# Four layers of attention on one core: two weight loads moved behind the opening stage, a dearer load in the planner, and a newly searched order

## The chip, the cores and the metric

The kernel is one program on one core of a Trainium2 chip. The core has a matrix engine (PE; its weight loads have a row of their own, PEld), a vector engine (DVE), a scalar engine (ACT), GpSimd (POOL) and SyncE (SP), which here does nothing but issue DMAs. Each engine takes its instructions in the order written, and waits for others at semaphores. The metric is the device time of one execution in microseconds (us); 495.82 us is the median of three runs of the kernel before (495.67 to 497.61).

## The reference

A token block x of 2048 x 512 (bf16) goes through two rounds of two layers, each added to x:

```python
x = A_x
x = x + _A_ref(_layernorm(x, axis=-1), A_wq, A_wk, A_wv, A_wo, A_beta)
x = x + _B_ref(_layernorm(x, axis=-1), B_wqkv, B_w_phi, B_wo)
x = x + _A_ref(_layernorm(x, axis=-1), A_wq, A_wk, A_wv, A_wo, A_beta)
x = x + _B_ref(_layernorm(x, axis=-1), B_wqkv, B_w_phi, B_wo)
```

Layer A is attention with a memory: 32 heads of width 16, four segments of 512 tokens. In each segment it forms q, k and v, takes a causal softmax attention within the segment, mixes it by a gate with what a running memory (a sum over earlier segments of phi(k) times v) returns for phi(q), and multiplies the result by `A_wo`. Layer B is linear attention: q and k are each multiplied per head by a 16 x 16 matrix `w_phi`, softmaxes of the product and of its negative are the features, and features of all keys times v are summed over all 2048 tokens before any query is answered; the result is multiplied by `B_wo`.

## The kernel before

**Stages.** x stays on the core as sixteen tiles `X` of 128 tokens. For each of four segments the program does: layer norm (`ln`: statistics on DVE, line 1099, the root on POOL, line 1105, the scaling on DVE, line 1114), a transpose of the normed tile `xn` into `xnT`, the projections of layer A (`a_proj`: keys `KT` and `KTo` for even and odd heads, queries `QT`, values `VT`, and `PhiK`/`PhiQ`), attention in pairs of tiles (`a_att`: score matmuls, exponentials of 1024 columns on ACT in lines 1289, 1300 and 1310, masks on POOL in line 1316 and DVE in line 1320, the product with `VT`), the output projection (`a_out`, `WA_o`), then layer B's norm, keys (`b_keys`: `WB_k`, `WB_v`, exponentials `Ek`) and queries (`b_queries`). Layer B's output (`b_out`, `WB_o`) can begin only when all four segments have gone through `b_keys`. Then the second round does the same, its first stage lying beside the end of the first round.

**The opening stage.** Before the first segment the inputs come in. `setup` issues the first four tiles of x and the weights of layer A in halves on the queues of ACT and SP; `late_loads` (line 1030) issues the rest on SP: the other twelve tiles of x, `w_phi`, the raw q and k weights of layer B (into the tiles `EQ`), `WA_o`, the value weight `WB_v` and the output weight `WB_o` of layer B, 512 KB each. `fold_weights` (line 1070) multiplies layer B's q and k weights by `w_phi` once, into `WB_q` and `WB_k`: each of eight 128-row pieces of `EQ` is transposed by a DMA into a tile `OT` (`transposed`, line 867; the DMA itself is line 860), multiplied on PE with the block matrix `wbd` (a tile `O`), and copied out of PSUM by ACT or DVE.

**The queue of SP.** All transposes by DMA, all loads on SP and all stores stand in one queue in a fixed order. A transpose waits at its place until the engine that makes its input has done so, and everything behind it waits too. In this trace what SP issues in the opening lands in the order of its issue.

**What sets the order.** Nothing is written out in the order in which it runs. `Program.add` records each operation with what it reads and writes; `PLAN` gives each of the 3474 operations its rank, `sequence` makes one list of them that respects the dependences, and each engine gets its part of the list. `ON` says for operations that could run on ACT, DVE or POOL which one takes them. `schedule` then walks through the lists with a cost for each operation: it decides which tile of a pool and which PSUM bank an operation gets, and puts idle matmuls (`warm`, line 1585) on PE where it expects a gap of at least one of them or where the share of time that PE is busy in the last `WIN` = 3.4 us would fall below `LOW`. `PAIRS` names score matmuls that are issued interleaved with the ones behind them. A DMA has a cost on the queue that issues it (0.5 us for a load, 1.28 for a transpose, line 863), a time on the rings (`weight`), and an `at`, the earliest time at which the planner lets it start. `at` puts no wait into the program: what is left of it on the chip is the DMA's place in the order.

The functions that the change touches:

Of the kernel before, what the change touches and what calls it, by code (L numbers as in the profile page):

```python
# [31 lines left out]
LOW = 0.39  # L32
# [11 lines left out]
    165, 213, 219, 241, 255, 269, 275, 281, 293, 297, 299, 307, 319, 325, 563, 585, 591, 609, 627, 670, 694, 696, 698, 702, 720, 722, 724, 728, 734,  # L44
    746, 748, 754, 961, 963, 985, 991, 1003, 1021, 1027, 1039, 1068, 1070, 1074, 1082, 1094, 1100, 1102, 1108, 1120, 1124, 1128, 1134, 1146, 1148,
    1150, 1152, 1154, 1351, 1392, 1410, 1422, 1451, 1455, 1465, 1477, 1481, 1505, 1511, 1517, 1529, 1531, 1533, 1537, 1543, 1784, 1790, 1844, 1868,
    1870, 1874, 1900, 1906, 1922, 1924, 1926, 1932, 1944, 1948, 1950, 1952, 2215, 2245, 2269, 2292, 2294, 2296, 2298, 2300, 2322, 2326, 2350, 2352,
    2370, 2378, 2384, 2639, 2651, 2657, 2669, 2687, 2693, 2718, 2730, 2748, 2756, 2774, 2776, 2794, 2796, 2800, 2802, 3021, 3023, 3046, 3064, 3082,
    3123, 3151, 3157, 3163, 3181, 3183, 3207, 3215, 3331, 3333,
# [8 lines left out]
    0, 5, 1, 6, 41, 43, 10, 8, 12, 11, 60, 27, 7, 66, 30, 29, 34, 31, 49, 350, 115, 44, 75, 65, 74, 83, 68, 94, 42, 16, 15, 26, 17, 25, 18, 22, 14,  # L58
    13, 62, 46, 48, 73, 80, 63, 106, 54, 55, 39, 121, 99, 67, 96, 118, 51, 57, 64, 32, 76, 56, 85, 72, 21, 78, 24, 71, 82, 89, 92, 70, 58, 28, 79,
    133, 135, 137, 111, 101, 151, 169, 181, 180, 38, 47, 35, 45, 37, 36, 33, 52, 50, 87, 97, 90, 77, 110, 53, 9, 122, 102, 91, 130, 120, 140, 40, 59,  # L60
    104, 81, 206, 244, 290, 142, 109, 23, 95, 134, 108, 143, 103, 107, 154, 124, 2, 164, 128, 69, 160, 177, 88, 131, 114, 158, 201, 196, 229, 217,
    153, 282, 295, 171, 231, 197, 243, 198, 175, 84, 148, 98, 19, 20, 147, 344, 353, 366, 360, 376, 157, 4, 112, 113, 179, 3, 105, 182, 168, 183, 193,
    172, 149, 185, 210, 208, 187, 163, 207, 209, 235, 212, 184, 191, 218, 273, 204, 248, 224, 144, 155, 245, 256, 253, 292, 268, 239, 289, 166, 116,
    226, 165, 214, 260, 286, 246, 194, 188, 213, 284, 265, 215, 324, 200, 343, 340, 351, 358, 294, 216, 269, 304, 328, 330, 335, 319, 312, 323, 308,
    342, 367, 354, 241, 384, 394, 402, 389, 364, 438, 454, 434, 442, 274, 211, 310, 270, 337, 336, 278, 141, 203, 242, 311, 288, 317, 258, 232, 297,
    322, 267, 375, 176, 349, 383, 281, 327, 387, 380, 396, 406, 414, 371, 400, 261, 411, 325, 359, 238, 392, 178, 390, 233, 422, 401, 298, 315, 357,
    374, 329, 386, 339, 326, 363, 420, 382, 399, 431, 447, 436, 279, 412, 262, 479, 368, 437, 362, 421, 369, 473, 487, 449, 453, 419, 285, 468, 403,
    443, 474, 501, 504, 481, 510, 450, 440, 537, 558, 497, 506, 518, 240, 482, 478, 466, 280, 472, 439, 503, 528, 441, 448, 470, 455, 524, 477, 569,
    559, 522, 575, 584, 579, 616, 433, 661, 673, 614, 634, 205, 234, 129, 86, 220, 223, 299, 159, 252, 117, 174, 152, 125, 127, 186, 170, 222, 93,
    332, 150, 355, 348, 318, 408, 361, 195, 250, 397, 385, 372, 356, 381, 266, 404, 410, 484, 499, 461, 415, 391, 416, 398, 379, 377, 202, 428, 427,  # L70
    417, 345, 407, 145, 429, 432, 313, 247, 287, 493, 446, 425, 395, 489, 430, 517, 451, 471, 476, 418, 465, 502, 459, 346, 293, 271, 277, 513, 512,
    333, 500, 494, 458, 539, 444, 485, 555, 561, 556, 545, 593, 625, 393, 365, 409, 136, 192, 126, 119, 199, 259, 219, 237, 291, 307, 296, 309, 283,
    228, 254, 139, 146, 306, 303, 320, 314, 331, 347, 316, 321, 457, 464, 452, 463, 475, 460, 490, 276, 492, 300, 638, 690, 644, 699, 688, 645, 715,
    630, 717, 632, 531, 520, 538, 542, 435, 567, 469, 649, 534, 519, 456, 547, 530, 557, 554, 580, 585, 551, 566, 553, 532, 495, 774, 787, 526, 650,
    769, 793, 755, 752, 801, 797, 808, 796, 788, 602, 651, 764, 677, 779, 726, 802, 800, 768, 833, 848, 851, 838, 850, 871, 855, 866, 863, 1339, 1313,
    1166, 1172, 1290, 1284, 1048, 1247, 1275, 1265, 1150, 1209, 1352, 1341, 1424, 1317, 1580, 1434, 1459, 1064, 1634, 1543, 1632, 1641, 647, 657, 671,
    730, 639, 680, 540, 710, 721, 693, 703, 564, 598, 563, 562, 582, 488, 508, 509, 511, 521, 523, 491, 480, 533, 334, 544, 560, 424, 496, 570, 445,
    586, 576, 568, 594, 606, 505, 591, 467, 610, 612, 583, 543, 572, 529, 622, 574, 552, 426, 629, 615, 603, 635, 654, 666, 601, 498, 643, 617, 483,
    627, 587, 516, 648, 590, 652, 664, 663, 682, 678, 675, 549, 691, 653, 588, 641, 637, 667, 656, 676, 619, 659, 697, 662, 668, 685, 621, 636, 705,
    701, 698, 738, 613, 708, 804, 813, 825, 744, 577, 514, 605, 527, 679, 548, 620, 486, 707, 550, 735, 660, 696, 525, 669, 700, 716, 728, 686, 592,  # L80
    681, 757, 713, 714, 718, 689, 758, 766, 782, 785, 658, 611, 794, 626, 749, 694, 628, 573, 720, 571, 781, 772, 776, 736, 751, 684, 771, 759, 795,
    665, 816, 805, 829, 832, 843, 834, 820, 824, 791, 798, 810, 783, 831, 823, 830, 837, 799, 864, 754, 780, 809, 822, 778, 777, 733, 731, 875, 868,
    880, 807, 881, 872, 883, 899, 845, 692, 846, 859, 890, 727, 844, 762, 888, 885, 878, 817, 722, 672, 750, 737, 775, 773, 917, 877, 847, 927, 884,
    876, 842, 536, 608, 999, 957, 1012, 993, 156, 100, 264, 301, 272, 251, 373, 370, 352, 123, 162, 167, 189, 255, 161, 275, 305, 138, 515, 388, 581,
    578, 541, 600, 546, 646, 607, 640, 655, 985, 988, 936, 840, 1003, 943, 742, 748, 765, 642, 674, 624, 597, 702, 338, 719, 723, 596, 740, 711, 747,
    695, 767, 784, 595, 589, 623, 790, 729, 763, 341, 806, 631, 818, 760, 743, 819, 828, 683, 839, 873, 841, 599, 604, 633, 704, 709, 724, 741, 745,
    753, 670, 761, 609, 867, 869, 378, 803, 897, 865, 712, 725, 706, 786, 835, 836, 734, 739, 746, 849, 792, 857, 756, 976, 947, 980, 974, 932, 1004,
    954, 860, 992, 1051, 903, 931, 821, 934, 920, 961, 1086, 1033, 968, 905, 963, 909, 904, 770, 858, 894, 889, 946, 915, 910, 925, 916, 1089, 1092,
    862, 955, 1140, 1102, 1043, 1110, 1088, 1044, 1101, 1090, 1065, 930, 1046, 1122, 1135, 1096, 1097, 1123, 1145, 1126, 1205, 1104, 1181, 1200, 1234,
    1212, 1098, 1094, 965, 986, 1118, 1108, 972, 891, 1115, 1148, 938, 973, 1163, 1159, 1197, 1210, 1198, 1187, 1136, 1078, 1263, 1268, 1572, 1435,  # L90
    1034, 1063, 1056, 1158, 1130, 1151, 1129, 1156, 1127, 1149, 1157, 902, 861, 907, 896, 852, 1079, 941, 1000, 967, 1084, 919, 1077, 1105, 1007,
    1008, 1072, 970, 1070, 1062, 1016, 939, 1053, 1054, 1038, 1083, 1138, 1117, 1107, 913, 1100, 1125, 1066, 1057, 1142, 923, 1144, 1128, 1047, 1112,
    1168, 1164, 1184, 1193, 1119, 1173, 1196, 1215, 1171, 1133, 1194, 1055, 1155, 978, 1190, 1203, 1177, 1175, 1223, 1162, 1229, 1232, 1189, 1141,
    1217, 1206, 1180, 1174, 1170, 1236, 1199, 1216, 1204, 1191, 1231, 1176, 1226, 1201, 1235, 1253, 1182, 1160, 1147, 959, 1041, 1296, 1311, 1314,
    1299, 956, 949, 900, 882, 995, 908, 998, 1013, 982, 983, 971, 811, 912, 887, 854, 964, 945, 826, 911, 898, 893, 906, 1006, 1009, 1005, 997, 1025,
    535, 1058, 926, 1029, 870, 1030, 1031, 1021, 987, 1017, 1024, 950, 928, 1018, 962, 944, 937, 1042, 892, 1035, 1068, 922, 1037, 1045, 1026, 1080,
    901, 1116, 1109, 1052, 1001, 1111, 1040, 1082, 984, 1087, 924, 1019, 895, 1015, 1069, 1036, 1011, 940, 853, 948, 981, 989, 1010, 1095, 1081, 1146,
# [187 lines left out]
class Program:  # L285
# [22 lines left out]
    def R(self, *key):  # L308
        r = self.fixed.get(key)
        if r is None:  # L310
            r = self.fixed[key] = Res()
        return r
# [505 lines left out]
class Kernel:  # L818
# [39 lines left out]
    def dma(self, dst, src, reads, writes, eng="sp", transpose=False, took=0.3, at=0.0):  # L858
        if transpose:
            f = lambda e: e.dma_start(dst(), src(), transpose=True)  # L860
# [770 lines left out]
```

## Time and profile before

| what | value |
|---|---|
| runs | 495.67, 495.82, 497.61 us |
| the profiled execution | 497.49 us, of which the span of the profile is 495.8 us |
| busy | PE 465.4 us, DVE 439.1, ACT 427.8, POOL 267.4 |
| mean granted clock of PE | 0.985 |
| chain that ended last | PE 44%, ACT 27%, DVE 22%, DMA 4% |
| DMA | 31.15 MB in 99156 packets, 90880 of them under 512 B |
| largest groups | exponentials L1310 and L1300 on ACT, 130.0 and 128.7 us; masks L1316 on POOL, 105.8 and 55.3 us |

The profile tells one execution. Its page has the busy time of the engines, the span in 40 slices of 12.4 us, the chain of work followed back from the end, and groups of like instructions. The trace behind it can be asked for each engine's instructions in order of time, for who waited for whom, and for busy times and the granted PE clock in any window. A wait for several semaphores is put down to the one that came last by the records, so a wait laid to an instruction that ended at another moment may be one for a DMA. The profiled execution is 1.67 us above the median of the runs.

### The profile page before, as it was taken

What the parts mean: (1) busy time and instruction counts of PE and PEld (TensorE: products, weight loads), DVE (VectorE), ACT (ScalarE), POOL (GpSimd) and SP (SyncE); (2) the same over time, 40 slices, a digit from 0 to 9 for tenths busy, and PEclk for the clock granted to TensorE, in tenths of its full rate; (3) what the DMA queues carried; (4) which work ended last, traced back from release to release, by engine and by line L of the source; (5) the groups of instructions that cost most, each with busy time, mean ns of one, the idle gap of its engine ahead of it and who ended that gap; (6) DMA issues with size and microseconds to landing.
All of it is one profiled execution on the core that took longest, in us unless ns stands there. A gap on an engine that the chain in (4) does not pass through costs nothing.

```text
span 495.8 us, 18863 instructions
## 1 busy us (share of the span) xinstructions
PE 465.4 (94%) x8039; PEld 311.1 (63%) x8127; DVE 439.1 (89%) x975; ACT 427.8 (86%) x594; POOL 267.4 (54%) x536
## 2 busy tenths in 40 slices
PE   7979999999998999999999999999999999999896
PEld 6647566666557655747767565667665667475653
DVE  6976999999878999799999999999998787879784
ACT  5868999999999999984799999999999999968142
POOL 4554539484457578341255457575776365635152
PEclk9977999999999999999999999999999999999999
DMA  8995554421230321100134553332415221110134
GB/s 234 245 121 112 85 76 77 66 52 28 47 54 15 56 45 23 28 4 4 29 60 67 65 82 78 60 65 56 78 32 67 35 48 27 22 27 2 41 74 124
DMA packets 99156, 31.15 MB, mean 63 GB/s; under 512 B 90880, under 2 KB 99072, under 8 KB 99072
## 3 DMA queue, kind: packets, MB, share of 16 engines
q1 hardware_dynamic: 97824, 28.88, 33.5%
q8 instruction: 64, 1.05, 0.9%
q10 hardware_dynamic: 1248, 1.06, 0.7%
q14 instruction: 20, 0.16, 0.1%
HBM read 6.32 MB, written 2.10 MB: 17 GB/s over the span
## 4 chain that ended last, share of the span: by engine, by line
PE 44%; ACT 27%; DVE 22%; DMA 4%; issue 2%; POOL 0%; ACTq 0%; SPq 0%
PE PS L798 41%; ACT PT L1300 10%; ACT DT L1310 8%; DVE stats L1099 3%; DMA OT<-O 2%; DVE DT L1320 2%; ACT Ek L1391 2%; ACT phi L1129 2%; ACT PT L1289 2%; DVE X L1363 2%; DVE O L1346 1%; PE PS L876 1%; PE PS L1585 1%; DVE Zk L1392 1%; DVE QT L854 1%
## 5 line engine op out<-in xcount | busy, mean ns | idle before, releaser
L1316 POOL TENSOR_SCALAR_AFFINE_SELECT DT<-DT 128x256 bf16<-128x256 bf16 (+1 forms) x256 | 105.8, 431 | 84.7 <-ACT DT L1310 41.7
L1310 ACT ACTIVATE DT<-PS 128x1024 bf16<-128x1024 f32 x128 | 130.0, 1049 | 5.6 <-PE PS L798 5.0
L1300 ACT ACTIVATE PT<-PS 128x1024 bf16<-128x1024 f32 x128 | 128.7, 1040 | 2.8 <-PE PS L798 2.3
L798 PE MATMUL PS<-VT,DT 128*128 128x17 bf16 x1536 | 77.9, 171 | 0.7 <-POOL DT L1316 0.4
L798 PE MATMUL PS<-QT,KT 32*64 32x64 bf16 (+3 forms) x1280 | 73.5, 224 | 5.3 <-ACT PT L1289 0.8
L1316 POOL TENSOR_SCALAR_AFFINE_SELECT DT<-PT 128x256 bf16<-128x256 bf16 x128 | 55.3, 444 | 42.5 <-DVE DT L1320 17.1
L798 PEld LDWEIGHTS PS<-VT,DT 128*128 128x128 bf16 x1536 | 71.2, 96 | 8.0 <-POOL DT L1316 0.7
L1397 POOL TENSOR_TENSOR Ek<-Ek,rZ 128x512 bf16<-128x512 bf16 x60 | 62.6, 1061 | 22.5 <-DVE rZ L1394 21.8
L798 PEld LDWEIGHTS PS<-QT,KT 32*128 32x128 bf16 (+1 forms) x1280 | 38.7, 98 | 49.6 <-ACT DT L1310 12.9
L798 PE MATMUL PS<-QT,KTo 32*64 32x64 bf16 (+3 forms) x1280 | 66.5, 218 | 0.0
L798 PEld LDWEIGHTS PS<-VT,PT 128*128 128x128 bf16 x1024 | 48.2, 96 | 8.7 <-issue 1.1
L798 PE MATMUL PS<-VT,PT 128*128 128x17 bf16 x1024 | 51.3, 171 | 0.2 <-ACT PT L1300 0.2
L1320 DVE TENSOR_TENSOR DT<-PT,late 128x256 bf16<-128x256 bf16 x128 | 41.7, 341 | 5.1 <-PE PS L798 4.1
L1099 DVE BATCH_NORM_STATS2 stats<-X 128x6 f32<-128x512 bf16 x64 | 43.6, 686 | 1.1 <-DMA X<-in_A_x_dram 0.2
L1105 POOL TENSOR_TENSOR rstd<-rstd,negh 128x2 f32<-128x2 f32 (+1 forms) x36 | 24.6, 683 | 31.7 <-DVE rstd L1103 29.4
L1392 DVE TENSOR_REDUCE Zk<-Ek 128x64 f32<-128x1024 bf16 x32 | 38.5, 1202 | 2.1 <-ACT Ek L1391 1.6
L798 PEld LDWEIGHTS PS<-QT,KTo 32*128 32x128 bf16 (+1 forms) x1280 | 39.5, 100 | 0.2
L1391 ACT ACTIVATE Ek<-PS 128x512 bf16<-128x512 f32 x64 | 35.3, 635 | 3.2 <-PE PS L798 3.0
L798 PE MATMUL PS<-xnT,WA_q 128*128 128x128 bf16 x512 | 35.1, 219 | 0.0
L1289 ACT ACTIVATE PT<-PS 128x1024 bf16<-128x1024 f32 x32 | 32.9, 1048 | 1.5 <-PE PS L798 1.4
L798 PE MATMUL PS<-WA_v,xnT 128*128 128x512 bf16 x110 | 31.7, 393 | 2.4 <-issue 1.5
L798 PE MATMUL PS<-WA_o,OT 128*128 128x512 bf16 x118 | 30.8, 380 | 2.5 <-issue 0.5
(146 smaller groups left out, 1000.9 us busy)
## 6 DMA issues: line engine op xcount, KB each, us to landing
EQ<-in_B_wqkv_dram SPq DMA_DIRECT2D x2, 512.0 KB, 9.0
out_dram<-X SPq DMA_DIRECT2D x8, 128.0 KB, 2.0
out_dram<-X SPq DMA_DIRECT2D x16, 64.0 KB, 2.0
X<-in_A_x_dram SPq DMA_DIRECT2D x6, 128.0 KB, 8.1
X<-in_A_x_dram SPq DMA_DIRECT2D x3, 256.0 KB, 8.4
OT<-O SPq DMA_TRANSPOSE x46, 2.5
xnT<-xn SPq DMA_TRANSPOSE x36, 2.6
WB_o<-in_B_wo_dram SPq DMA_DIRECT2D x1, 512.0 KB, 8.8
```

Source lines behind the costliest of these rows:

```text
L798: return e.matmul(o, l, r, start=st, stop=sp, tile_position=(basep(l), basep(o)))
L1099: self.dve(lambda e, t=t: e.bn_stats(self.stats[:, t, :], self.X[:, t, :]), 0.60, [R("X", t)], [R("stats", t)])
L1105: self.pool(lambda e, ve=ve, n=n: e.tensor_tensor(ve, ve, self.negh[:, 0:1].to_broadcast([128, n]), ALU.pow), 0.76, [R("rstd", t0 + i) for ...
L1129: self.act(lambda e: e.activation(shape(t2.ap), src(), ACT.Exp), 512, [res()], [t2()])
L1289: self.act(lambda e, st=st, pt=ta[y]: e.activation(pt.ap[:].rearrange("p b c -> p (b c)"), self.ps[:, st.slot[0] * 512:st.slot[0] * 512 + ...
L1300: self.act(lambda e, st=st, pt=pt: e.activation(pt.ap[:].rearrange("p b c -> p (b c)"), self.ps[:, st.slot[0] * 512:st.slot[0] * 512 + 102 ...
L1310: self.act(lambda e, st=st, dt=dt: e.activation(dt.ap[:, :, :, 64:320], self.ps[:, st.slot[0] * 512:st.slot[0] * 512 + 1024].rearrange("p ...
L1316: lambda e, c=c, src=src, base=base, p=p, block=block: e.affine_select(block(c, p), src() if src else block(c, p), [[0, 2], [0, 2], [1, 64 ...
L1320: P.add(("dve",), lambda e, early=early, block=block: e.tensor_tensor(block(320), early(), self.late[:, None, None, :].to_broadcast([128, ...
L1391: self.act(lambda e, sgn=sgn, Ek=Ek, gen=gen: e.activation(Ek.ap[:, sgn, :], self.bank(gen), ACT.Exp, scale=1.0 - 2.0 * sgn), 512, [gen()] ...
L1392: self.dve(lambda e, Ek=Ek, Zk=Zk: e.tensor_reduce(Zk.ap[:], Ek.ap[:].rearrange("p s (h j) -> p s h j", h=H), AX.X, ALU.add), 1.15, [Ek(0) ...
L1397: P.add(("dve", "pool") if late else ("pool",), lambda e, Ek=Ek, rZ=rZ, sgn=sgn: e.tensor_tensor(Ek.ap[:, sgn, :].rearrange("p (h j) -> p ...
```

## The change

Five edits:

- In `late_loads` the loads of `WA_o`, `WB_v` and `WB_o` get an earliest time in the plan: 44.9, 46.0 and 70.0 us.
- In `dma` a load costs the issuing queue 0.62 us in the plan, instead of 0.5.
- `LOW` goes from 0.39 to 0.42.
- `PLAN` is another table throughout, found by a new search from the old one; `PAIRS` has 170 members instead of 136, of which 87 are common.
- `ON` moves some copies between ACT and DVE: ACT gets 113 of its listed operations instead of 117, DVE 104 instead of 100.

```diff
-LOW = 0.39
+LOW = 0.42
...
 PAIRS = {
...
-    0, 5, 1, 6, 41, 43, 10, 8, 12, 11, 60, 27, 7, 66, 30, 29, 34, 31, 49, 350, 115, 44, 75, 65, 74, 83, 68, 94, 42, 16, 15, 26, 17, 25, 18, 22, 14,
...
-        op = self.P.add(eng, f, 1.28 if transpose else 0.5, reads, writes, lat=1.5 if transpose else 1.3, isdma=True)
+        op = self.P.add(eng, f, 1.28 if transpose else 0.62, reads, writes, lat=1.5 if transpose else 1.3, isdma=True)
...
-        self.load("sp", self.WA["o"][:], self.wview(inp["A_wo"]), [R("WA", "o")], 1.6)
-        self.load("sp", self.WB["v"][:], self.wview(wqkv[:, 1024:1536]), [R("WB", "v")], 1.6)
+        self.load("sp", self.WA["o"][:], self.wview(inp["A_wo"]), [R("WA", "o")], 1.6, at=44.9)
+        self.load("sp", self.WB["v"][:], self.wview(wqkv[:, 1024:1536]), [R("WB", "v")], 1.6, at=46.0)
         x_rows(2)
         x_rows(3)
-        self.load("sp", self.WB["o"][:], self.wview(inp["B_wo"]), [R("WB", "o")], 1.6)
+        self.load("sp", self.WB["o"][:], self.wview(inp["B_wo"]), [R("WB", "o")], 1.6, at=70.0)
```

What this makes of the queue of SP, from the programs as built (places in the queue; T is a transpose):

```
before                                      after
16  WB_o                                    14  T PhiK
17  T PhiK                                  15  T OT<-EQ  (4)
18  WB_v                                    19  T OT<-EQ
19  T OT<-EQ  (4)                           20  T PhiK
23  T PhiK                                  21  T OT<-EQ
24  T OT<-EQ  (2)                           22  T xnT
26  T xnT                                   23  T OT<-EQ, xnT, OT<-EQ, PhiK (2), xnT (4)
27  T OT<-EQ, xnT, OT<-EQ, PhiK (2),        32  T KTo, xnT
      xnT (3)                               34  WA_o
35  WA_o                                    35  T OT<-O
36  T xnT, KTo, xnT, OT<-O (2), KT ...      36  WB_v
                                            37  T OT<-O, KT, KTo, KT, xnT (2), EQ ...
                                            55  WB_o
                                            56  T KTo, KT, KTo ...
```

Nearer the start, SP's half of `WA_v` also moves: it stood right behind SP's half of `WA_q`, ahead of two loads of x and the first `EQ`, and now stands behind these three. The number of instructions of every kind on PE is the same in both programs, 154 idle matmuls among them; they stand at other places.

## The prediction

> **What bounds the kernel now.** I read the forty slices first, to see whether one engine is full throughout.
>
> ```profile
> PE   7979999999998999999999999999999999999896
> ACT  5868999999999999984799999999999999968142
> PEclk9977999999999999999999999999999999999999
> ```
>
> PE is full nearly everywhere, but a busy PE is not a fast one: the third row says that PE got 0.7 of its clock in slices 2 and 3 (24.8 to 49.6 us) and 0.9 or more everywhere else. So I cut the opening into windows (us, then PE, PEld, DVE, ACT, POOL busy, the clock, DMA share, GB/s).
>
> ```profile
> 14.00:28.40 14.40, 12.21 (x206) 9.05 (x205) 14.12 (x35) 13.48 (x19) 8.48 (x20) 1.00 1.28 210
> 28.40:30.20 1.80, 1.53 (x16) 1.03 (x17) 1.80 (x9) 0.06 (x1) 1.36 (x4) 1.00 1.04 208
> 30.21:43.86 13.65, 12.59 (x170) 8.00 (x170) 7.14 (x20) 9.36 (x12) 5.18 (x13) 0.50 0.54 90
> 43.86:46.50 2.64, 2.59 (x43) 1.80 (x42) 2.18 (x5) 2.01 (x3) 2.42 (x7) 1.00 0.25 50
> 50.00:200.00 150.00, 142.93 (x2723) 93.62 (x2750) 139.10 (x312) 146.80 (x193) 94.33 (x193) 1.00 0.31 51
> ```
>
> For 13.65 us PE ran at half speed. It was busy for 12.59 of them while ACT had 9.36 of work, 69%; from 50 to 200 us ACT is at 97.9%, so there ACT bounds, and whatever time ACT loses earlier is added to the end. What slowed PE? Its rows in order of time, idle before each in brackets:
>
> ```profile
> 25.58 1.07 PE L798 MATMUL PS<-xnT,WA_q 128*128 128x128 bf16 x16
> 28.67 0.47 PE L798 MATMUL PS<-O,OT 128*128 128x128 bf16 x4 [2.02 <-DVE phi L1131]
> 32.53 0.61 PE L798 MATMUL PS<-O,OT 128*128 128x128 bf16 x4 [0.50 <-DMA OT<-EQ]
> ```
>
> A hole of 2.02 us before the first fold matmul, and the clock goes at 30.21. The hole is laid to DVE, but by the program's order this matmul waits for a DMA as well, the second transpose of `EQ`. The queue of SP:
>
> ```profile
> 14.73 1.78 SPq L862 DMA_DIRECT2D WB_o<-in_B_wo_dram  x1
> 16.55 2.03 SPq L860 DMA_TRANSPOSE PhiK<-phi  x1
> 18.64 0.58 SPq L862 DMA_DIRECT2D WB_v<-in_B_wqkv_dram  x1
> 19.26 7.62 SPq L860 DMA_TRANSPOSE OT<-EQ  x4
> ...
> 26.93 1.26 SPq L860 DMA_TRANSPOSE PhiK<-phi  x1
> ```
>
> That second transpose (issued at 22.1) has this landing time:
>
> ```profile
> DMA to landing us min/median/max: 6.4/6.4/6.4
> ```
>
> It landed at 28.5, and PE started at 28.67: the DMA ended the hole. It sat behind `WB_o` (landed at 14.73 + 8.8 = 23.5) and `WB_v` (18.64 + 8.1 = 26.7). ACT's waits from 28 to 46.5 us follow:
>
> ```profile
> ACT DT L1310 <- PE PS L798: 2.0, 2, 1.4
> ACT phi L1129 <- DMA PhiK<-phi: 1.8, 1, 1.8
> ACT WB_k L854 <- PE PS L798: 1.4, 1, 1.4
> ACT VT L854 <- PE PS L798: 1.0, 1, 1.0
> ACT PT L1289 <- PE PS L798: 0.4, 1, 0.4
> ```
>
> All are for the slow PE or for a transpose behind the loads. The chain of waits agrees; its longest opening pieces from 28 us on are that queue and the slow PE:
>
> ```profile
> 28.23 4.25 DMA OT<-EQ
> ...
> 35.23 4.53 PE PS L798 x49
> ```
>
> **The change, part by part.**
>
> *Two loads leave the opening queue.* SP saves 1.78 + 0.58 = 2.36 us of issue before the fold transposes. On the rings they hold up what follows from 22.0 (last x load landed, 14.1 + 7.9) to 26.7, with one transpose between; that transpose still takes its 1.9 (23.5 to 25.4), so transposes of `EQ` land about 28.5 - 3 = 25.5, before PE ends its projection at 26.65. The hole goes. What is late next is DVE, which is full from 14 to 31.9 with the statistics of x; the new order has the same sixteen of them by then, so nothing before 28 us gets earlier: I count zero there. Behind it ACT has 0.06 + 9.36 + 2.01 = 11.43 us of work in the 18.1 us from 28.4 to 46.5. At its rate in the window before (13.48 of 14.40, 93.6%) this takes 12.2 us: 5.9 saved, the upper end. DVE has 1.80 + 7.14 + 2.18 = 11.12 us there, at 92.7% (139.10 of 150) 12.0 us, so it allows as much. PE's 12.59 us of half-speed work is 6.3 at full speed; with 1.53 + 2.59 it needs 10.4. The lower end, if the hole goes: the 1.8 us wait for the DMA, and half of ACT's 4.8 us of waits for PE, 2.4, since PE is twice as fast: 4.2. Below that lies the case that the clock falls all the same (a rival). I take 4.6, nearer to the lower end, because of SP: it issues a transpose only every 1.27 us, seventeen of them stand between the last load of x and `WA_o`, and this queue gets shorter by the loads' 2.36 us for sure and by at most the 3.3 us more that the transposes in their wake took over 1.27 each (2.03 - 1.27 and 7.62 - 4 x 1.27), 2.4 to 5.7, 4.0 in the middle.
>
> The Trainium skill (TensorE: Matmul & The Clock Gate, "What's actually happening") says that the gate halves the clock after an idle window of about 3.4 us, counted in free-running windows. The 13.65 us here are four such windows, which agrees; but a hole of 2.02 us was enough in this trace, so the page's bare rule, by which only holes over 3.4 us matter, would make the clock safer in the new order than I count it.
>
> *The loads land elsewhere.* `WA_o` keeps its place near 45 us; `WB_v` comes two places behind it, `WB_o` some twenty places on. A load holds up the transposes behind it: `xnT` behind `WA_o` took 5.5 us to land against a median of 2.6, 2.9 more.
>
> ```profile
> DMA to landing us min/median/max: 5.5/5.5/5.5
> ```
>
> Two new loads: 0 to 5.8 us of delay to the transposes of the next segment's keys. What hides it: those keys landed from 58.1 to 60.7 here, and the next segment's first score exponential ran at 65.9, 5.2 us later, with other ACT work between. I take 0 and keep 5.8. A gain from this side is excluded but for the one counted. The loads' own users are far: `WB_v` first at 69, `WB_o` at 232.
>
> *`WA_v` later.* Its half lands about where the first `EQ` did, 13.6 instead of 10.2. Its first matmul stood at 13.8; the new order puts a transpose group, 16 score matmuls and three idle ones ahead of it. 0, at most 0.5.
>
> *0.62 and `LOW`* act through the order alone. The idle matmuls are 154 in both; no cost, except where they stand.
>
> *Copies move.* ACT loses four instructions of 0.60 us (-2.4), DVE gains four of 0.68 (+2.7). ACT is at 97.9%, DVE at 92.7%, so between -2.4 and +2.7; I take 0, the two rows being equally near.
>
> *The new order and pairs.* A group of eight paired score matmuls spans 0.42 us (25.23 to 25.65) against 0.40 for four unpaired (18.76 to 19.16), so a pair spares PE 0.4 us, 34 pairs 13 us; but ACT bounds and the pair waits for two free PSUM tiles. No row prices an order. What it can win is ACT's idle time in the two full stretches (3.2 us of 50 to 200, 4.5 of 250 to 400), what it can lose is as much: I take 0, and 3 either way.
>
> Sum: -4.6. The profiled execution (497.49; span 495.8 and 1.69 around it) is 1.67 above the median of the runs. The gain is time of the span, so it comes off either: 495.8 - 4.6 = **491.2**.
>
> **The rivals.**
>
> *A: the clock holds, the order is neutral*: as summed, 495.8 - 5.9 - 1.1 to 495.8 - 4.2 + 1.7, that is 488.8 to 493.3 with a little of the order's 3 us on either side.
>
> *B: the clock falls anyway.* DVE is full until 31 us, and PE's first fold and key matmuls also wait for DVE and ACT to empty PSUM; another hole of 2 us drops the clock there. Against it: the new order has eight key matmuls on both sides of the first fold and fourteen idle matmuls right behind the second. Then only the 1.8 us wait goes, and three of four slow windows may stay: 494, between 493.3 and 497. The Trainium skill's free-running window (same page) would make this a matter of chance in each execution; before, three runs lie within 1.94 us, so the drop came in all or in none.
>
> *C: slower, by transposes behind the loads at 45 to 60 us.* `WA_o` and `WB_v` are parted by one transpose, and keys and `xnT` of the next segments stand behind. Three loads at 2.9 are 8.7 us of delay. It decides where more than 4.6 + 2.5 of this is on the path; all of it gives 495.8 - 4.6 + 8.7 = 499.9, and with the gain lost too, more. Against it stand the 5.2 us of slack.
>
> *D: the order wins too*: the 3 us in full, 486 to 488.8.
>
> **How the numbers follow.** A 0.59, B 0.18, C 0.17, D 0.06. Half a per cent, 2.5 us, is about what a measurement here can tell from no change: faster is below 493.3, slower above 498.3. Faster is nearly all of A, and D: 0.63. Same is B and a little of A and C: 0.21. Slower is most of C: 0.16. The range goes from 488.5 to 498.0: below it lies D, 0.06, above it most of C, 0.14. The likeliest case alone: 488.8 to 493.3.
>
> **What would show it.** Right: no slow clock between 25 and 50 us; the first fold matmul without a hole before it; transposes of `EQ` landing near 25.5; ACT in 28.4 to 46.5 above 85%; the state that before had at 46.5 reached near 42. Step C wrong: landing times of transposes behind `WB_v` above 5 us with PE or ACT waiting for a `KT`, `KTo` or `xnT`. The forecast falls if the clock row shows a slow stretch of three or four windows anywhere, or if ACT's idle time between 50 and 400 grows beyond 12 us.

## The result, and the profile after

The changed kernel took 491.95 us, the median of four executions (491.37 to 492.46), against 496.0 for the kernel before beside it (four, 495.67 to 497.61): a ratio of 0.9912, 95% interval 0.9887 to 0.9937. Six more executions on a later occasion had a median of 493.03 against 496.03, a ratio of 0.9935 (0.9911 to 0.9959). By these two ratios it is faster by 0.65 to 0.9%, 3 to 4 us. The profiled execution took 492.46 us, with a span of 490.7.

The forty slices of the kernel after, PE, ACT and the granted clock:

```profile
PE   7998999999999999999999999999999999999896
ACT  4998999999999999783899999999999998968142
PEclk9999999999999999999999999999999999999999
```

The dent in the clock in slices 2 and 3 is gone. In windows (us; PE, PEld, DVE, ACT, POOL busy; clock; DMA share; GB/s), the kernel after:

```profile
14.00:28.40 14.40, 13.86 (x253) 10.19 (x248) 13.82 (x34) 13.80 (x19) 11.58 (x26) 1.00 1.21 171
28.40:46.50 18.10, 15.98 (x334) 10.97 (x332) 15.88 (x47) 16.25 (x22) 8.58 (x22) 1.00 0.52 85
50.00:200.00 150.00, 145.86 (x2790) 93.60 (x2778) 138.35 (x303) 145.61 (x192) 94.70 (x192) 1.00 0.34 56
```

In the second window ACT did 16.25 us of work, where it had done 11.43: 4.8 us more by 46.5 us, and the profiled time is 5.0 lower. From 50 to 200 us ACT's work changed little (145.61 of 150, before 146.80). So the gain lies where the sum had put it. PE around the first fold matmul, in order of time:

```profile
25.71 0.40 PE L799 MATMUL PS<-O,OT 128*128 128x128 bf16 x4
...
27.15 0.39 PE L799 MATMUL PS<-O,OT 128*128 128x128 bf16 x4
27.37 1.69 PE L1586 MATMUL PS<-warm 128*128 128x256 bf16 x14
```

No idle time stands in brackets before it; it ran at 25.71 instead of 28.67. The queue of SP shows why, and where the loads went:

```profile
14.28 1.29 SPq L861 DMA_TRANSPOSE PhiK<-phi  x1
15.62 8.31 SPq L861 DMA_TRANSPOSE OT<-EQ  x5
...
45.06 0.59 SPq L863 DMA_DIRECT2D WA_o<-in_A_wo_dram  x1
45.70 1.19 SPq L861 DMA_TRANSPOSE OT<-O  x1
46.93 0.59 SPq L863 DMA_DIRECT2D WB_v<-in_B_wqkv_dram  x1
47.56 1.19 SPq L861 DMA_TRANSPOSE OT<-O  x1
```

Transposes start where `WB_o` stood. The second of `EQ` was issued at 17.76 and landed at 24.70 (before: 22.1 and 28.5). Of ACT's waits between 28.4 and 46.5 us one is left; the 1.8 us for the DMA of `PhiK` is gone:

```profile
ACT PT L1301 <- PE PS L799: 1.7, 1, 1.7
```

One thing got worse, at 47 to 58 us. The chain of waits there:

```profile
46.93 0.59 SPq L863
47.52 0.04 issue
47.56 5.99 DMA OT<-O
53.56 0.05 issue
53.60 3.23 PE PS L799 x34
```

The transpose of `O` behind `WB_v` took 6.0 us to land, and the output projection waited for it. To see what that cost, take the start of the n-th exponential of 1024 elements a partition on ACT, in the two profiled executions (counted from the trace):

| n, counted from 0 | before | after | lead |
|---|---|---|---|
| 0 | 13.71 | 14.21 | -0.5 |
| 14 | 42.58 | 35.46 | 7.1 |
| 20 | 51.04 | 45.04 | 6.0 |
| 30 | 61.77 | 55.31 | 6.5 |
| 32 | 63.57 | 58.14 | 5.4 |
| 106 | 159.00 | 153.91 | 5.1 |
| 287, the last | 437.06 | 432.83 | 4.2 |

Seven us are won by 42 us. About one is gone again by n = 20 (ACT's wait of 1.7 us shown above, which ends at 41.13), another goes between n = 30 and n = 32, and another in the long rest.

### The profile page after: what moved, and what is told of

It is laid out like the page before. It is cut to its first block, busy times and chain, and to the rows that moved or that the text cites. A ratio compares the mean times of both kernels' runs of the same rounds, so it can differ in the third digit from the quotient of the medians.

```text
span 490.7 us, 18973 instructions
## 1 busy us (share of the span) xinstructions
PE 470.4 (96%) x8127; PEld 307.3 (63%) x8127; DVE 441.6 (90%) x979; ACT 425.7 (87%) x590; POOL 268.4 (55%) x536
## 4 chain that ended last, share of the span: by engine, by line
PE 47%; ACT 24%; DVE 22%; DMA 4%; issue 2%; ACTq 1%; POOL 0%; SPq 0%; DVEq 0%
PE PS L799 44%; ACT DT L1311 7%; ACT PT L1301 7%; DMA OT<-O 3%; DVE DT L1321 3%; ACT PT L1290 2%; ACT phi L1130 2%; DVE stats L1100 2%; DVE X L1364 2%; DVE PhiQ L1134 1%; PE PS L1586 1%; DVE O L1347 1%; DVE xn L1115 1%; PE PS L877 1%; DVE phi L1132 1%
## 5 line engine op out<-in xcount | busy, mean ns | idle before, releaser
L1317 POOL TENSOR_SCALAR_AFFINE_SELECT DT<-DT 64x256 bf16<-64x256 bf16 (+1 forms) x256 | 106.5, 436 | 72.2 <-ACT DT L1311 29.8
L1398 POOL TENSOR_TENSOR Ek<-Ek,rZ 128x512 bf16<-128x512 bf16 x60 | 62.3, 1055 | 25.1 <-DVE rZ L1395 22.1
L799 PE MATMUL PS<-QT,KTo 32*64 32x64 bf16 (+3 forms) x1280 | 65.3, 216 | 0.0
L799 PE MATMUL PS<-WA_v,xnT 128*128 128x512 bf16 x128 | 34.8, 380 | 0.2
L799 PE MATMUL PS<-WA_o,OT 128*128 128x512 bf16 x128 | 32.8, 380 | 1.5 <-DMA OT<-O 0.8
```

The lines of the kernel that those rows point to most:

```text
L799: return e.matmul(o, l, r, start=st, stop=sp, tile_position=(basep(l), basep(o)))
L1317: lambda e, c=c, src=src, base=base, p=p, block=block: e.affine_select(block(c, p), src() if src else block(c, p), [[0, 2], [0, 2], [1, 64 ...
L1398: P.add(("dve", "pool") if late else ("pool",), lambda e, Ek=Ek, rZ=rZ, sgn=sgn: e.tensor_tensor(Ek.ap[:, sgn, :].rearrange("p (h j) -> p ...
```

## The experiments

My theory: the loads' leaving the opening queue makes the whole gain, mostly by way of the clock, and the new order is neutral. The rivals: the order makes it; or the late transposes cost the time by themselves, and the clock little. The two transplants below edit SP's queue behind the planner (`put` takes an operation out of the queue and sets it behind another), so that every other engine's order is untouched. The code shown is cut to the lines that matter (`...`); the comments are added.

### The loads alone, in the old order

```diff
         self.span = P.schedule()
...
+        put(self.load_wbv, sp(4))                      # behind the fourth operation after WA_o
+        put(self.load_wbo, P.ops[q[q.index(self.load_wbv.i) + 19]])
```

> The kernel before, with every engine's order as it was, and only WB_v and WB_o moved in the queue of SP: WB_v behind the first transpose of layer A's output at about 45 us, WB_o some nineteen places on. Theory (the loads hold up the transposes of EQ, the hole of 2.02 us drops the PE clock): the hole shrinks to what VectorE alone makes it wait, under 1 us (its own last release of that PSUM bank ended at 27.5), the clock stays full from 25 to 50 us, and the time falls by 3 to 5 us, to 491 to 493. Rival (the newly searched order makes the gain, not the loads): the time stays within 1 us of the kernel before, 495 to 497.

492.33 us (nine executions), ratio 0.9931 (0.9912 to 0.995). Between 28.4 and 46.5 us:

```profile
28.40:46.50 18.10, 17.11 (x343) 12.02 (x341) 16.16 (x46) 16.74 (x23) 12.30 (x30) 1.00 0.65 112
```

The old order with the loads moved has nearly all of it: 3.7 us of the 4.05 of the result. Its mean (492.3) and that of all ten executions of the changed kernel (492.5) differ by 0.2, so the new order, the new pairs and the moved copies together are worth nothing that can be seen (0.2 us with about 0.9 either side), given that the loads come late.

### The loads put back, in the new order

```diff
         self.span = P.schedule()
...
+        put(self.load_wbo, lead)       # ahead of the first transpose of PhiK
+        put(self.load_wbv, P.ops[first])   # and right behind it
```

> The changed kernel, with every engine's order as it is, and only WB_o and WB_v put back in the queue of SP around the first transpose of PhiK, where they stood before. Theory: transposes of EQ land near 28 instead of 25, the first fold matmul waits 2 us or more, the PE clock falls to half for three or four windows of 3.4 us, and the time rises by 3 to 6 us over the changed kernel, to 495 to 498. Rival (new order makes the gain): within 1.5 us of the changed kernel, 491 to 493.5.

494.41 us (ten executions), ratio 0.9969 (0.9944 to 0.9993): about 2 us lost again. Neither expectation was met; the time lies between them. Seen from this side the loads are worth 2.0 us (means 494.5 and 492.5) and the rest of the change 1.6 (496.0 and 494.5): the new order stands the loads in the opening better than the old one does, and which part of it does so was not tried. Its second transpose of `EQ` landed at 27.6, and the clock fell for one window instead of four:

```profile
PEclk9989999999999999999999999999999999999999
```

### The hole filled, the loads left where they were

This is meant to give the old kernel its clock back and nothing else: 14 idle matmuls in PE's hole ahead of the first fold matmul.

```diff
+        f = P.idle_op(P.ops[i].done, 14, bank, 0.0)
...
+        q.insert(p, f.i)               # q: PE's queue, p: place of the first fold matmul
```

> The kernel before, loads where they were, with 14 idle matmuls (256 columns each) put ahead of the first fold matmul, so that PE is busy through the hole. Theory that the clock is the larger part: clock full from 30 to 44 us, the time falls by 2 to 4 us, to 492 to 494; what stays is ScalarE's wait of 1.8 us for the transpose of phi behind the loads. Rival (late landing itself is the cost, the clock only goes along with it): less than 1 us gained, 495 to 497.

495.28 us (ten executions), ratio 0.9995 (0.9977 to 1.0013): next to nothing. Over the ten executions the mean clock rose only from 0.9954 to 0.9969, so the times alone do not price the clock. In the profiled execution the hole is closed and the clock stays at 1.0:

```profile
26.80 1.70 PE L1586 MATMUL PS<-warm 128*128 128x256 bf16 x14 [0.31 <-ACT DT L1311]
28.39 0.38 PE L798 MATMUL PS<-O,OT 128*128 128x128 bf16 x4
...
31.79 0.40 PE L798 MATMUL PS<-O,OT 128*128 128x128 bf16 x4 [0.95 <-DMA OT<-EQ]
```

But the transposes are as late as they were, and ACT waits for them. Its longest wait between 28.4 and 46.5 us, and the two pieces of the chain:

```profile
ACT phi L1130 <- DMA PhiK<-phi: 3.0, 1, 3.0
```

```profile
26.64 4.50 DMA PhiK<-phi
...
34.88 4.98 DMA OT<-EQ
```

```profile
28.40:46.50 18.10, 15.07 (x299) 10.62 (x298) 13.14 (x37) 13.71 (x18) 10.15 (x24) 1.00 0.72 98
```

Read the windows of the three kernels together. At full clock with late transposes ACT did 13.71 us of work, with early ones 16.74: 3.0 us, and the mean times at full clock are 2.8 apart (next section). From the slow clock to the full one it went from 11.43 to 13.71: 2.3 us, and the profiled execution of before (497.49) is 2.4 above its executions at full clock. So the clock was the smaller part even in that execution, which was a bad one: by these windows about 2.3 us, against 3.0 for the late transposes.

### The clock from execution to execution

I had one profile of before, at a clock of 0.985, and took that for its rule. Each execution's mean clock says otherwise. Mean time by mean granted clock (number of executions; the 58 of before ran on three chips, with means of 495.9 to 496.3):

| kernel | 0.998 to 1.0 | 0.995 to 0.997 | below 0.995 | all |
|---|---|---|---|---|
| before | 495.1 (14) | 495.9 (24) | 496.8 (20) | 496.0 (58) |
| before, hole filled | 495.0 (3) | 495.6 (7) | | 495.5 (10) |
| before, `WB_v` moved | 494.0 (6) | | 495.9 (5) | 494.9 (11) |
| before, `WB_o` moved | 493.3 (6) | 494.2 (3) | 494.8 (2) | 493.8 (11) |
| before, both moved | 492.3 (9) | | | 492.3 (9) |
| after | 492.1 (8) | 494.1 (2) | | 492.5 (10) |
| after, loads put back | | 494.2 (8) | 495.5 (2) | 494.5 (10) |

A straight line through the 58 executions of before gives 495.05 at full clock and 0.21 us for each 0.001 lost; one slow window of 3.41 us is 0.0034 of the span, 0.7 us. The mean loss of before is 0.0046, so by this line the clock costs it 1.0 us on average. The line shows that clock and time go together, not which brings the other. The other 2.8 (495.1 to 492.3, with 0.7 either side) is there at full clock.

A mean does not say where the clock was lost. In the profiled execution with `WB_o` moved (0.997) all of the loss lies in the last 2.64 us of the span, behind PE's last matmul, and the opening kept its clock. So the columns of the table part the executions only roughly.

The program is the same each time; how much of the clock it loses changes from execution to execution. The Trainium skill (TensorE: Matmul & The Clock Gate, "What's actually happening") has the windows free-running, which agrees with this. Its idle window of about 3.4 us as the condition does not fit: in before a hole of 2.02 us preceded the drop, and a later execution of the kernel after lost the window from 39.79 to 43.21 us with PE idle for no more than 1.09 us before 38.67 and 0.31 before 39.85. The profiled execution of the result had nearly the same holes there (0.92 and 0.33) and kept its clock.

Where a hole falls matters. In these traces the clock changes only on a grid of 3.41 us. The kernel with 13 idle matmuls cut (below) has two profiled executions, and in both PE has the same hole of 1.7 us up to 29.35. In one it lies within one stretch of the grid, 26.96 to 30.38 us, in which PE was busy for 1.71 us; the next stretch was slow. In the other a boundary of the grid at 28.52 parts it, PE was busy for 2.29 and 2.58 us in the two stretches, and the clock stayed. PE's busy time alone is no rule: 2.06 us preceded the slow stretch from 39.79, and 1.91 (loads put back, 40.06 to 43.48) preceded none. In before the slow clock lasted until a stretch in which PE was busy throughout; it was busy for 2.91 to 3.19 us in the three slow ones ahead of that.

### One load at a time

```diff
...
+        put(self.load_wbv, sp(4))      # the first kernel; WB_o stays
...
+        put(self.load_wbo, sp(23))     # the second kernel; WB_v stays
```

> The kernel before with WB_v alone put behind WA_o on SP's queue; WB_o stays where it was. Both loads moved gave 492.3 against 496.0, a gain of 3.7 us. Three theories share these 3.7 us out differently. (1) The gain is the time on SP's queue: the share of WB_v is its issue time, 0.58 of 2.36 us, so 0.9 us: 495.1. (2) The gain is the time on the rings: the two loads' landings (8.1 and 8.8 us behind their issue) are about equal, so half, 1.8 us: 494.2. (3) What counts is whether the second transpose of EQ lands before PE ends its projection at 26.65 us: the last bytes ahead of it are gone with WB_v, it lands near 25.5 to 26.5, the hole is closed and nearly all is won: 492.3 to 493.2, with the granted clock at 1.0.

494.71 us (eleven), ratio 0.9979 (0.9958 to 0.9999).

> The kernel before with WB_o alone put some twenty places behind WA_o on SP's queue; WB_v stays where it was. (1) Time on SP's queue: 1.78 of 2.36 us, so 2.8 us of the 3.7: 493.2. (2) Time on the rings: half, 1.8 us: 494.2. (3) Landing before 26.65 us: WB_v is issued 1.78 us earlier and starts on the rings when the last load of x is in at 22.0, lands near 24.5, and the second transpose of EQ near 26.3, so the hole is closed as well: 492.3 to 493.2. If (3) holds, the two halves are not additive: each alone gives nearly the whole.

493.62 us (eleven), ratio 0.9962 (0.9945 to 0.9979).

By the medians `WB_v` is worth 0.94 us and `WB_o` 2.03, together 2.97 of the 3.7 of both. At full clock it is 1.1 and 1.8, and 2.8 for both. So the parts roughly add up, and theory (3), by which each alone gives nearly the whole, falls by `WB_v`, whose interval ends at 2.1 us. Between (1), issue time on SP (0.9 and 2.8), and (2), equal halves (1.8 and 1.8), the numbers lie about midway and do not decide: the intervals are 0.0 to 2.1 and 1.0 to 2.7 us, so the halves fit both, and of the issue times 2.8 lies just outside. The profiles can't say how the load's time becomes the loss. Those three executions were all near full clock, took much the same time (493.19 with `WB_v` moved, 493.4 with `WB_o`, 493.37 with both), and PE's hole ahead of the first fold matmul was 0.93 us in each. `WB_v` alone moved, then both (that execution starts 0.6 us later throughout):

```profile
27.59 0.40 PE L798 MATMUL PS<-O,OT 128*128 128x128 bf16 x4 [0.93 <-DVE O L1346]
```

```profile
28.19 0.40 PE L798 MATMUL PS<-O,OT 128*128 128x128 bf16 x4 [0.93 <-DVE O L1346]
```

So (3) describes the profiled executions, and not the others: with `WB_v` moved the profiled one is the fastest of eleven, and five lost over 0.005 of the clock. What the landings were in those isn't known. In the profiles the row of transposes behind is later with one load left: the fourth of `EQ` landed at 27.82 with `WB_v` moved, 27.64 with `WB_o` moved, 26.45 with both.

### The us given back at 47 to 58 us

```diff
...
+        put(self.load_wbv, P.ops[q[q.index(self.load_wbv.i) + 6]])   # where SP's queue waits
```

> The changed kernel with WB_v six places further back on SP's queue, where SP waits from 55.70 to 58.11 us; WB_v is first used at 63.33. In the changed kernel the transpose of O behind WB_v took 6.0 us to land (47.56 to 53.56), the output projection waited 0.84 us for it, and ACT 0.87 us for PE at 58.14; the lead over the kernel before fell by 1.0 us there. Theory: that 1.0 us is the price of WB_v's place and lasts to the end; the transpose lands 2 us earlier and the time is 490.8 to 491.2. Rival: ACT would have lost it a little later anyway (the plan's order is tight behind), the time stays at 491.95 within 0.4. Second rival: WB_v now lands near 59.5 and holds up the transposes of xn issued at 58.11: 492.5 or more.

492.34 us (six), ratio 0.9926 (0.9902 to 0.9951). In the profiled execution the place did what was expected of it. SP's queue, and the landing time of the second transpose of `O`, 3.2 us instead of 6.0:

```profile
45.40 2.50 SPq L861 DMA_TRANSPOSE OT<-O  x2
...
55.44 0.58 SPq L863 DMA_DIRECT2D WB_v<-in_B_wqkv_dram  x1
57.17 2.50 SPq L861 DMA_TRANSPOSE EQ<-xn  x2
```

```profile
DMA to landing us min/median/max: 3.2/3.2/3.2
```

ACT's exponential at the end of that stretch, in the kernel after and here:

```profile
58.14 1.02 ACT L1311 ACTIVATE DT<-PS 128x1024 bf16<-128x1024 f32 x1 [0.87 <-PE PS L799]
```

```profile
57.21 1.02 ACT L1311 ACTIVATE DT<-PS 128x1024 bf16<-128x1024 f32 x1
```

The wait is gone, 0.9 us are won there, and 1.0 us of lead is kept to the last exponential. Still, the mean of the six (492.25) is only 0.2 below that of the ten of the kernel after, with 1.2 us between single executions (one standard deviation). One us is what one execution showed; in the times it is not resolved.

### Fewer idle matmuls, and what beats both kernels

The run of 14 idle matmuls behind the second fold matmul, cut to 1, in the kernel after:

```diff
-            for _ in range(n):
+            for _ in range(1 if n == 14 else n):
```

> The changed kernel, with the run of 14 idle matmuls behind its second fold matmul cut to one: a hole of about 1.8 us opens on PE at 27.6 with no other work moved. If a hole of near 2 us is enough wherever it lies, the clock falls after it and the time rises by 3 to 5 us, to 495 to 497. If it takes a hole within one window of 3.4 us, some executions fall and some do not (mean clock 0.985 against 1.0 in the same kernel), with times in two groups. If this hole is too short, the time is unchanged, 491.5 to 492.5.

490.94 us (four), ratio 0.9908 (0.9876 to 0.9941), at clocks of 0.993 to 0.997. The clock did fall, in the profiled execution for one window from 30.38 us, and the rise of 3 to 5 us that was expected with it did not come.

The same cut with `WB_v` and `WB_o` both issued where SP's queue waits:

```diff
...
+        put(self.load_wbv, P.ops[q[q.index(self.load_wbv.i) + 6]])
+        put(self.load_wbo, P.ops[q[q.index(self.load_wbo.i) - 5]])
```

> As the last one, and WB_o five places earlier, where SP waits from 70.10 to 72.16 us (the transpose of ktoko behind it took 5.7 us to land, 78.90 to 84.56), and the run of 14 idle matmuls at 27.37 us cut to 1, which alone gave 490.9 against 491.95 without the difference being resolved. Theory, the two add up: 490.0 within 0.4. Rival, no more than one of them is real: 490.9 to 491.9. A slow window of the clock near 30 us is expected, as with the cut alone, at 0.9 us.

489.95 us (six), ratio 0.9883 (0.9861 to 0.9906). To share this out, the four combinations were run on one chip:

> The changed kernel itself, beside three variants of it on one chip, so that differences near 1 us can be read. 491.95 as on record, within 0.5; granted clock 0.998 to 1.0.

> The changed kernel with the run of 14 idle matmuls at 27.37 us cut to 1 and nothing else; it gave 490.94 in four executions, 1.0 us below the changed kernel on another occasion, and lost one window of the clock in each. Theory: the 13 idle matmuls cost PE some 1.5 us while ACT waits for its scores, more than the lost window costs (0.9 us by the spread of the kernel before): 491.0 within 0.4, below the first run of this call. Rival: the 1.0 us was chance, both times agree within 0.3.

> The changed kernel with WB_v and WB_o issued where SP's queue waits (near 55.7 and 70.1 us) and the 14 idle matmuls kept. With WB_v alone so placed, the profiled execution had 1.0 us more of lead at the 287th exponential, but the median of six was 492.3. Theory: the 1.0 us is real: 491.0 within 0.4. Rival: it is one execution's, and the time is that of the changed kernel within 0.3.

> Both edits, 489.95 in six executions. If both are real and add up: 490.0, 1.9 below the first run of this call. If only the cut is real, this equals the run with the cut alone; if only the loads' places are, it equals the run with them alone, in both cases about 1 us above 489.95.

| kernel | on this chip: median, ratio | mean of all executions |
|---|---|---|
| after | 493.03 (6), 0.9935 (0.9911 to 0.9959) | 492.5 (10) |
| cut | 491.5 (6), 0.9917 (0.989 to 0.9943) | 491.55 (10) |
| loads in the gaps | 492.36 (6), 0.9926 (0.9899 to 0.9953) | 492.5 (6) |
| both | 490.71 (4), 0.989 (0.9872 to 0.9908) | 490.3 (10) |

Both edits together are 2.15 us below the kernel after, with an interval of about 0.9 either side (from the spread of ten executions each): a version that beats both kernels. The cut alone (-0.9 with 1.2 either side) and the loads' places alone (0.0) are not resolved. How they add up stays open. Here the kernel after came out 1.1 us above its first median, more than the 0.5 expected, and the cut and the loads' places stayed 0.5 and 1.4 us above the 491.0 of their theories.

One source of the spread can be seen. Up to 37.88 us ACT keeps the same times within 0.01 us in four profiled executions: the two of the kernel after, and those of the cut and of the loads in the gaps on this chip; then it waits for scores that stand behind the key projection on PE, which waits for a transpose of `xn`. This wait is 1.74 us in the kernel after in the result's profile, 2.94 in its later one, 0.68 with the cut:

```profile
41.13 1.02 ACT L1301 ACTIVATE PT<-PS 128x1024 bf16<-128x1024 f32 x1 [1.74 <-PE PS L799]
```

```profile
42.34 1.02 ACT L1301 ACTIVATE PT<-PS 128x1024 bf16<-128x1024 f32 x1 [2.94 <-PE PS L799]
```

```profile
40.08 1.02 ACT L1301 ACTIVATE PT<-PS 128x1024 bf16<-128x1024 f32 x1 [0.68 <-PE PS L799]
```

In the second of these the key projection itself ran in the slow window that began at 39.79, 1.86 us instead of 1.02:

```profile
39.85 1.86 PE L799 MATMUL PS<-WA_k,xnT 128*128 128x512 bf16 x4 [0.31 <-DMA xnT<-xn]
```

The third of these is early because its row of transposes was: the one that ended the wait was issued at 34.23, in the first at 35.41. That is not shown to be the cut's doing. In the three other profiled executions with the cut the row was issued at 35.31 to 35.77, and in one without it (`WB_v` where SP's queue waits) at 34.64.

## Why the prediction was right, and where it was not

- **The total**: 491.2 forecast, 491.95 measured, inside the likeliest case's own range (488.8 to 493.3). Rival A came about.
- **Two loads leave the opening queue**: right. Moved alone they made 3.7 of 4.05 us. The second transpose of `EQ` landed at 24.70 (forecast 25.5), the hole is gone, ACT was at 89.8% between 28.4 and 46.5 (above 85%). What before had reached at 45.64 (n = 16 above) the kernel after reached at 37.9, earlier than the "near 42" of the forecast, of which some 3 us were given back.
- **The clock as the main term**: wrong in size. The sum led its reader to the half-speed stretch; of the lower end of 4.2, 2.4 was the clock's. With the hole filled and the transposes left late, the gain was 0.7 us by the medians, and nothing that the interval separates from none; at full clock the two kernels take 495.0 and 495.1. The terms that were too small are the late landings themselves: 1.8 us for one wait of ACT, where the kernel with the hole filled waits 3.0, and PE another 0.95. The queue's own bound, 2.4 to 5.7 us, was the one that named the mechanism; 2.8 lies in it, though which part of the queue's time it is, issue or landing, stays open. The sum was made against an execution whose clock loss was unusually large (0.015 against a mean of 0.0046). That the total came out so near was in part luck: the clock was put too high, the late landings too low, and the two made up for each other.
- **"The drop came in all or in none"**: wrong. Times within 1.94 us of each other do not show that: one slow window is worth 0.7 us. 14 of 58 executions lost less than 0.0025 of the clock, 20 more than 0.005.
- **Loads landing elsewhere, rival C**: the mechanism was right, and the 0 that the sum took for it was not. The transpose behind `WB_v` took 6.0 us to land; PE waited 0.84 and ACT 0.87. I had looked for the cover in the next segment's keys, which kept 4.4 us of their 5.2 us of slack (55.18 to 59.58); the one late was a transpose of `O`, wanted at once by the output projection. About 1 us in the profiled execution, far from the 7.1 at which C would have decided.
- **`WA_v` later**: its half landed at 12.89, and the first exponential came 0.5 us later, the upper end; by the third it was regained.
- **The new order, pairs and copies at 0**: right as a whole with the loads late, 0.2 apart; with the loads in the opening the new order was worth 1.6. The 0.4 us for a pair was too high a price: it took the time that a group spans, where groups overlap. Unpaired groups follow each other 0.23 us apart (22.47 and 22.70 in before), and the paired one gives way to the next matmul after 0.35 (25.23 to 25.58), so a pair spares about 0.1. It entered the sum at 0. The copies, the dearer load and `LOW` were not tried one by one.
- **ACT's idle time from 50 us on**: 4.4 us of 50 to 200 and 4.6 of 250 to 400, where above 12 would have made the forecast fall. This reads the sign for the two full stretches of the sum; from 200 to 250 us ACT is idle for 13.6 us more, and was for 12.8 before.

## What to carry to other kernels

A load of weights that nobody needs for 40 us was not free in a queue that also carries transposes (2.8 us at full clock for two): look at who stands behind it. When a profile shows a stretch at half clock, find out whether the clock or the wait that brought it on is the cost, by filling the hole and leaving the wait; and look at several executions before taking one profile's clock for the kernel's. Compare work done by the bound engine at a fixed time, 46.5 us here: in the profiled executions of the kernel with its hole filled, with the loads put back, after, and with the loads moved it was 2.3, 2.9, 4.8 and 5.3 us above before, and the times 2.9, 3.1, 5.0 and 4.1 below.

## What the runs showed of the hardware that I had not expected

- The same program lost anything from none to 0.016 of its mean granted clock, and the time went with it, at about 0.21 us for each 0.001. Slow windows followed holes of 1.1 to 2.5 us on PE in some executions, and the same or nearly the same holes were followed by none in others.
- Losing a window was not seen to cost more than the idle matmuls that prevent it: with 13 of them cut the clock was lower (mean 0.9949 against 0.9991), and the time 0.9 us lower with 1.2 either side.
- A load of 512 KB held the transpose right behind it on SP's queue to 6.0 us from issue to landing, against 3.2 with the load elsewhere:

```profile
WB_v<-in_B_wqkv_dram SPq DMA_DIRECT2D x1, 512.0 KB, 4.7
OT<-O SPq DMA_TRANSPOSE x1, 6.0
```

- Executions that agree to 0.01 us up to 37.9 us part by 1.2 us within the next five (two profiles of the kernel after), over one row of transposes and one slow window.
